# One half of a score tile in every fourth block goes from ScalarE's exponential to GpSimd's power

## The chip, the cores and the metric

The kernel runs on one core of one Trainium2 chip. A core has five engines that each work through their own queue in order: TensorE (PE in the profile, with PEld for its weight loads), VectorE (DVE), ScalarE (ACT), GpSimd (POOL) and SyncE (SP), which here only issues DMAs. They wait for one another through semaphores. The metric is the device time of one execution in microseconds (us); lower is better.

## What is computed

Two branches read the same `x` (2048 rows of 512 numbers) and are mixed row by row with a sigmoid gate. Branch A is attention with 32 heads of width 16 that share one key and one value; branch B is a SwiGLU feed-forward layer of width 1792. All data are float32.

```
g = _sigmoid((x * gate_w).sum(-1, keepdims=True))
# A: attention
q = (x @ wq).reshape(B, S, 32, 16) ; k = x @ wk ; v = x @ wv
scores = einsum("bhqd,bkd->bhqk", q, k) * (Dh ** -0.5)
p = softmax(scores) ; a = einsum("bhqk,bkd->bhqd", p, v) @ wo
# B: feed-forward
b = (silu(x @ w_gate) * (x @ w_up)) @ w_down
return g * a + (1 - g) * b
```

Branch A needs one exponential for each of 32 x 2048 x 2048 scores. The kernel takes no maximum off the scores first; a bound on them is checked at the end, and a slower path that takes the maximum is entered only where the bound fails.

## The kernel before

**Stages.** A first stage (to about 50 us) transposes `x`, makes keys, values and the first queries. The main stage (to about 1260 us) runs attention and, interleaved with it on TensorE, the rest of the projections and the feed-forward. A last stage multiplies by `wo` and mixes the branches.

**Units and tiles of attention.** A unit `u` is one head and one piece of 128 keys (512 units, 16 to a head). Its scores against all 2048 queries are two score tiles, `j` = 0 and 1, of 128x1024 in PSUM (`pss`, two buffers, two banks each). Each becomes half of the unit's tile `pt` (128x2048, SBUF). `score` issues the two matmuls of a score tile (L660). `exps` exponentiates with ScalarE (L668, scale 0.25). `mix` multiplies a whole `pt` by the values and a column of ones and adds into `po` (L680); the ones give the softmax's denominator.

**Blocks.** From unit 32 on the work goes in blocks of four units (`block`, k = 8 to 127). In block k the score tiles of units 4k+2 to 4k+5 are made, numbered i = 0 to 7, and then units 4k to 4k+3 are mixed. So units 4k+4 and 4k+5, tiles 4 to 7, are mixed only at the end of the next block. The order of a block is written out by hand: `STEPS` says where a score tile (S) and where a step of the feed-forward (F) stands on TensorE; an F is a matmul on the lower 64 rows of the array beside one on the upper 64 rows.

**Staged halves.** `KINDS = "AHHAHAAA"` says how each of the eight tiles is exponentiated. An A tile goes from PSUM through ScalarE in one instruction of 128x1024. Of an H tile (i = 1, 2, 4) ScalarE takes the first 512 columns from PSUM ("d" in `EXPS`), while VectorE copies the other 512 raw scores from PSUM into `pt` (L664), so that PSUM comes free early; ScalarE later exponentiates that staged half in place, `pt<-pt` ("s" in `EXPS`). `EXPS = ("0d", "1d", "2d", "3d", "4d", "5d", "1s", "4s", "2s", "|", "6d", "7d")` is ScalarE's order; at "|" stand the tanh of the feed-forward, if one is due.

**The other engines.** VectorE also evacuates the feed-forward's results (`pf`), multiplies them together in SBUF (L284, L298), splits them into a rounded and a remainder part (`split`, L106 and L107), and after each head normalizes its output (L689 and L692). GpSimd does one thing in this stage: it splits every weight tile that a DMA has brought (`wraw`) into two parts, a cast (L106) and a subtraction (L107). It waits for the DMA and for the matmuls that still read the buffer. SyncE issues all DMAs in program order.

Of the kernel before, what the change touches and what calls it, by code (L numbers as in the profile page):

```python
# [1 line left out]

# [6 lines left out]
F32 = mybir.dt.float32  # L9
# [4 lines left out]
ALU = mybir.AluOpType  # L14
# [4 lines left out]
P = 128  # L19
# [7 lines left out]
CH = 512  # L27
# [7 lines left out]
SCALE = DH ** -0.5  # L35
# [13 lines left out]
BLOCK = 4  # L49
# [13 lines left out]
def tile_gated_mix(ctx, tc, x, wq, wk, wv, wo, w_gate, w_up, w_down, gate_w, out):  # L63
    nc = tc.nc
# [3 lines left out]
    cpool = ctx.enter_context(tc.tile_pool(name="cpool", bufs=1))  # L68
# [55 lines left out]
    def run(queue, n):  # L124
        for _ in range(min(n, len(queue))):
            queue.pop(0)()
# [506 lines left out]


    PO, LATER = [], []
    hp = tc.alloc_tile_pool(name="hp", bufs=2)
    with tc.tile_pool(name="bpool", bufs=2) as bp:
        PT = {}
# [14 lines left out]
        def score(u, j, half=False):  # L653
            h, kt = divmod(u, NT)
            if j == 0:
                new_pt(u)
            ps = ps_s.tile([P, 2 * CH], F32, name="pss")
            for b in range(2):
                rows = slice(b * RT, (b + 1) * RT)
                nc.tensor.matmul(ps[:, b * CH:(b + 1) * CH], ks[rows, kt * P:(kt + 1) * P], QS[h][rows, j, :],  # L660
                                 start=True, stop=True)
            halves.clock += 1
            pt = PT[u][:, j * 2 * CH:(j + 1) * 2 * CH]
            other = nc.vector.tensor_copy(pt[:, CH:], ps[:, CH:]) if half else None  # L664
            return pt, ps, other

        def exps(pt, ps, other=None, w=slice(None)):
            ins = nc.scalar.activation(pt[:, w], ps[:, w], AF.Exp, scale=SCALE)  # L668
            if other is not None:
                tc.declare_no_dep(getattr(ins, "ins", ins), getattr(other, "ins", other), reason="another bank")  # L670

        def mix(u):
            h, kt = divmod(u, NT)
            pt = PT.pop(u)
            if kt == 0:
                run(COPY, 1)
                PO[:] = [ps_o.tile([P, CH], F32, name="po")]
            po = PO[0]
            for c in range(NCH):
                nc.tensor.matmul(po[c * 2 * DH:(c + 1) * 2 * DH, :], vaug[:, kt, :], pt[:, c * CH:(c + 1) * CH],  # L680
                                 start=(kt == 0), stop=(kt == NT - 1))
            if kt == NT - 1:

                osb = hp.tile([P, CH], F32, name="osb")
                rsb = hp.tile([P, CH], F32, name="rsb", bufs=1)

                def invert(i):
                    w = slice(i * P, (i + 1) * P)
                    nc.vector.reciprocal(rsb[:, w], rsb[:, w])  # L689

                def store():
                    nc.vector.tensor_tensor(osb, osb, rsb, ALU.mult)  # L692
                    for c in range(NCH):
                        nc.sync.dma_start(o_d[h * DH:(h + 1) * DH, c * CH:(c + 1) * CH],
                                          osb[c * 2 * DH:c * 2 * DH + DH, :])

                assert not LATER
                COPY.append(lambda: nc.vector.tensor_copy(osb, po))
                LATER.extend([(0.8, lambda: nc.vector.stream_shuffle(rsb, osb, [DH] * 2 * DH))] +
                             [(1.0, lambda i=i: invert(i)) for i in range(TC)] + [(0.8, store)])  # L700
# [5 lines left out]
        def feed(k, more=True):  # L706
            for _ in range(k):
                if JOBS and more or halves.busy():
                    halves.step(more)

        def block(k, first, last, steps, kinds, order):
            more = k < NB - STOP
            tiles = [(u, j) for u in range(first, last) for j in range(2)]
            order = list(order)
            made = []

            def emit():
                while order and order[0] != "|" and int(order[0][0]) < len(made):
                    i, how = int(order[0][0]), order.pop(0)[1]
                    pt, ps, other = made[i]  # L720
                    if how == "s":
                        exps(pt, pt, w=slice(CH, None))
                    else:
                        exps(pt, ps, other, slice(0, CH) if kinds[i] == "H" else slice(None))

            for i, what in enumerate(steps):
                if what == "F":
                    if "S" in steps[i + 1:i + 3] and kinds[len(made):len(made) + 1] == "H":
                        HOLD.append(i)
                    feed(1, more)  # L730
                    HOLD.clear()
                elif len(made) < len(tiles):
                    made.append(score(*tiles[len(made)], kinds[len(made)] == "H"))
                    emit()
                    run(EVAC, len(EVAC))
                if len(made) > 4:
                    run(COPY, 1)
            if order:
                order.pop(0)
            run(ACTS, len(ACTS))  # L740
            emit()
            assert not order and len(made) == len(tiles)
            left = BUDGET
            rest = NT // BLOCK - k % (NT // BLOCK)
            for _ in range(-(-len(LATER) // rest) if DEFER else 2):
                if LATER:
                    cost, f = LATER.pop(0)
                    left -= cost
                    f()
            for last in (False, True):  # L750
                kept = set()
                for item in list(DEFER):
                    n, cost, f = item
                    if n in kept or (n in FRESH) != last or cost > left:
                        kept.add(n)
                    else:
                        DEFER.remove(item)
                        left -= cost
                        f()
            FRESH.clear()  # L760
            for u in range(BLOCK * k, BLOCK * (k + 1)):
                mix(u)
            halves.clock += 2 * LONG
# [92 lines left out]
    with tc.If(rv != 0):  # L856
        with tc.tile_pool(name="gpool", bufs=2) as gp:
            with tc.For_i(0, H, 1) as h:
# [3 lines left out]
                for qt in range(NT):  # L862
# [17 lines left out]
                    for b in range(NT // TC):  # L880
                        pt = ps_f.tile([P, CH], F32, name="pf")
# [48 lines left out]
```

## Time and profile before

| | |
|---|---|
| median of 2 runs (lowest to highest) | 1343.7 us (1343.49 to 1343.92) |
| the profiled execution, its own time | 1344.01 us |
| span of its instructions | 1341.9 us |
| VectorE, share of the span busy | 54% |
| ScalarE | 79% |
| GpSimd | 29% |
| GpSimd, instructions | 408 |

The profiled execution's own time is 2.1 us more than the span between its first and its last instruction. A row of a group gives the busy time of all its instructions, the mean of one in nanoseconds, then the time its engine sat idle before them and what ended it. A row of the timeline gives start, length, engine, line, operation, output and inputs, shape, the number of instructions merged, and in brackets the idle time before. Where one instruction's end overlaps the next one's start, the row shows both.

### The profile page before, as it was taken

What the parts mean: (1) busy time and instruction counts of PE and PEld (TensorE: products, weight loads), DVE (VectorE), ACT (ScalarE), POOL (GpSimd) and SP (SyncE); (2) the same over time, 40 slices, a digit from 0 to 9 for tenths busy, and PEclk for the clock granted to TensorE, in tenths of its full rate; (3) what the DMA queues carried; (4) which work ended last, traced back from release to release, by engine and by line L of the source; (5) the groups of instructions that cost most, each with busy time, mean ns of one, the idle gap of its engine ahead of it and who ended that gap; (6) DMA issues with size and microseconds to landing.
All of it is one profiled execution on the core that took longest, in us unless ns stands there. A gap on an engine that the chain in (4) does not pass through costs nothing. (4 is left out here: it accounts for less than half of the span.)

```text
span 1341.9 us, 26802 instructions
## 1 busy us (share of the span) xinstructions
PE 1328.0 (99%) x10743; PEld 770.4 (57%) x10743; DVE 722.4 (54%) x1221; ACT 1061.6 (79%) x1463; POOL 391.0 (29%) x408
## 2 busy tenths in 40 slices
PE   9999999999999999999999999999999999999997
PEld 7655555555555555555555555555555555555576
DVE  5554565555455555555464555455454565465432
ACT  4578888888888888888888888888888888888400
POOL 6140321152042151152131241142131241333343
PEclk9999999999999999999999999999999999999999
DMA  8455221131122221141131221231121221222154
GB/s 277 142 173 190 65 60 38 35 107 44 44 86 77 78 80 38 35 107 44 52 122 39 82 79 39 57 83 45 52 61 30 81 79 39 74 68 60 44 161 143
DMA packets 101489, 107.79 MB, mean 80 GB/s; under 512 B 9968, under 2 KB 69616, under 8 KB 99696
## 3 DMA queue, kind: packets, MB, share of 16 engines
q1 hardware_dynamic: 99632, 105.81, 27.5%
q8 instruction: 88, 1.44, 0.5%
q10 hardware_dynamic: 1728, 0.20, 0.1%
q14 instruction: 41, 0.34, 0.1%
HBM read 76.09 MB, written 29.36 MB: 79 GB/s over the span
## 5 line engine op out<-in xcount | busy, mean ns | idle before, releaser
L668 ACT ACTIVATE pt<-pss 128x1024 f32<-128x1024 f32 (+1 forms) x1024 | 842.0, 876 | 177.3 <-PE pss L660 146.3
L664 DVE COPY pt<-pss 128x512 f32<-128x512 f32 x354 | 244.8, 692 | 415.6 <-PE pss L660 380.6
L680 PE MATMUL po<-pt,vaug 128*32 128x512 f32 x4096 | 467.6, 595 | 0.0
L660 PE MATMUL pss<-qs,ks 64*128 64x512 f32 x2048 | 403.1, 417 | 1.1 <-ACT pt L668 1.1
L660 PEld LDWEIGHTS pss<-qs,ks 64*128 64x128 f32 x2048 | 193.7, 184 | 218.4 <-ACT pt L668 183.6
L680 PEld LDWEIGHTS po<-pt,vaug 128*32 128x32 f32 x4096 | 119.2, 109 | 260.2 <-issue 255.2
L668 ACT ACTIVATE pt<-pt 128x512 f32<-128x512 f32 x354 | 195.7, 620 | 0.0
L176 PE MATMUL pf<-xh,wgl 64*128 64x512 f32 (+1 forms) x440 | 162.0, 392 | 0.0
L176 PE MATMUL pf<-xh,wgh 64*128 64x512 f32 (+1 forms) x440 | 160.5, 391 | 0.5 <-DVE acc L331 0.2
L176 PE MATMUL pf<-xl,wgh 64*128 64x512 f32 (+1 forms) x440 | 160.2, 390 | 0.0
L176 PE MATMUL pf<-xh,wuh 64*128 64x512 f32 (+1 forms) x440 | 158.4, 391 | 0.7 <-DVE sign L403 0.3
L176 PE MATMUL pf<-xl,wuh 64*128 64x512 f32 (+1 forms) x440 | 158.2, 390 | 0.0
L176 PE MATMUL pf<-xh,wul 64*128 64x512 f32 (+1 forms) x440 | 157.3, 391 | 0.0
L106 POOL CAST wgh<-wraw 128x512 fp32r<-128x512 f32 x56 | 36.1, 644 | 402.6 <-PE pf L176 311.8
L176 PE MATMUL pf<-wdh,hh 64*128 64x512 f32 (+1 forms) x427 | 143.4, 391 | 1.7 <-DVE hh L106 1.7
L176 PE MATMUL pf<-wdh,hl 64*128 64x512 f32 (+1 forms) x427 | 144.1, 390 | 0.0
L176 PE MATMUL pf<-wdl,hh 64*128 64x512 f32 (+1 forms) x427 | 143.4, 390 | 0.0
L689 DVE RECIPROCAL rsb<-rsb 128x128 f32<-128x128 f32 x128 | 117.1, 935 | 10.1 <-issue 8.2
L106 POOL CAST wuh<-wraw 128x512 fp32r<-128x512 f32 x56 | 35.1, 626 | 298.2 <-PE pf L176 245.3
L176 PEld LDWEIGHTS pf<-xh,wgh 64*128 64x128 f32 (+1 forms) x440 | 78.5, 185 | 9.8 <-issue 2.5
L176 PEld LDWEIGHTS pf<-xh,wuh 64*128 64x128 f32 (+1 forms) x440 | 77.3, 185 | 9.3 <-issue 3.7
L176 PEld LDWEIGHTS pf<-xl,wgh 64*128 64x128 f32 (+1 forms) x440 | 78.5, 185 | 6.0
(157 smaller groups left out, 1547.6 us busy)
## 6 DMA issues: line engine op xcount, KB each, us to landing
wraw<-in_B_w_gate_dram SPq DMA_DIRECT2D x56, 256.0 KB
wraw<-in_B_w_up_dram SPq DMA_DIRECT2D x56, 256.0 KB
wraw<-in_B_w_down_dram SPq DMA_DIRECT2D x56, 256.0 KB
qs<-q_d SPq DMA_DIRECT2D x62, 192.0 KB
q_d<-hl SPq DMA_DIRECT2D x18, 256.0 KB
q_d<-hh SPq DMA_DIRECT2D x18, 256.0 KB
o_d<-osb SPq DMA_DIRECT2D x128, 32.0 KB
a_d<-acc SPq DMA_DIRECT2D x4, 1024.0 KB
```

The lines of the kernel that those rows point to most:

```text
L106: eng_hi.tensor_copy(hi, src)
L176: ins = nc.tensor.matmul(self.ps, a, b, start=(i == 0 and not half), stop=(last and half != 0))
L660: nc.tensor.matmul(ps[:, b * CH:(b + 1) * CH], ks[rows, kt * P:(kt + 1) * P], QS[h][rows, j, :], start=True, stop=True)
L664: other = nc.vector.tensor_copy(pt[:, CH:], ps[:, CH:]) if half else None
L668: ins = nc.scalar.activation(pt[:, w], ps[:, w], AF.Exp, scale=SCALE)
L680: nc.tensor.matmul(po[c * 2 * DH:(c + 1) * 2 * DH, :], vaug[:, kt, :], pt[:, c * CH:(c + 1) * CH], start=(kt == 0), stop=(kt == NT - 1))
L689: nc.vector.reciprocal(rsb[:, w], rsb[:, w])
```

## The change

A column `base` of 128 numbers, each e to the power SCALE (SCALE is 0.25), is made once. In blocks with k % 4 == 1 the staged half of tile 4 is no longer exponentiated by ScalarE; GpSimd raises `base`, read again for every column, to the power of the raw score: (e^0.25)^s = e^(0.25 s).

```diff
+import math
...
     PO, LATER = [], []
+    base = cpool.tile([P, 1], F32, name="base")
+    nc.vector.memset(base, math.exp(SCALE))
...
                     i, how = int(order[0][0]), order.pop(0)[1]
                     pt, ps, other = made[i]
-                    if how == "s":
+                    if how == "s" and i == 4 and k % BLOCK == 1:
+                        nc.gpsimd.tensor_tensor(pt[:, CH:], base.to_broadcast([P, CH]), pt[:, CH:], ALU.pow)
+                    elif how == "s":
                         exps(pt, pt, w=slice(CH, None))
```

This comes to 30 instructions (k = 9, 13, ... 125). The line numbers of the changed kernel are higher: by 1 up to the memset, by 3 in `score` and `mix`, and by more after that. On ScalarE 30 of the rows `ACTIVATE pt<-pt 128x512` are gone, always the middle one of three, and nothing else moves there. VectorE has one row more, the memset. SyncE's rows are the same.

GpSimd's queue around block k = 69, before the change (`wgh`, `wgl`, `wuh`, `wul` are the two parts of a gate and of an up weight tile, `wraw` what the DMA brought):

```order
L106 CAST wgh_8188<-wraw_8186 128x512 [waits DMAHW6_49,PE_49]
L107 TENSOR_TENSOR wgl_8189<-wraw_8186,wgh_8188 128x512 [waits PE_49,Pool_49]
L106 CAST wuh_8281<-wraw_8279 128x512 [waits DMAHW3_49,PE_49]
L107 TENSOR_TENSOR wul_8282<-wraw_8279,wuh_8281 128x512 [waits PE_49,Pool_49]
L106 CAST wgh_8372<-wraw_8370 128x512 [waits DMAHW4_49,PE_49]
L107 TENSOR_TENSOR wgl_8373<-wraw_8370,wgh_8372 128x512 [waits PE_49,Pool_49]
```

And the same place with the change:

```order
L107 CAST wgh_8190<-wraw_8188 128x512 [waits DMAHW6_49,PE_49]
L108 TENSOR_TENSOR wgl_8191<-wraw_8188,wgh_8190 128x512 [waits PE_49,Pool_49]
L107 CAST wuh_8283<-wraw_8281 128x512 [waits DMAHW3_49,PE_49]
L108 TENSOR_TENSOR wul_8284<-wraw_8281,wuh_8283 128x512 [waits PE_49,Pool_49]
L725 TENSOR_TENSOR pt_8297<-base_629,pt_8297 128x512 [waits DVE_49,Activation_49]
L107 CAST wgh_8374<-wraw_8372 128x512 [waits DMAHW4_49,PE_49]
L108 TENSOR_TENSOR wgl_8375<-wraw_8372,wgh_8374 128x512 [waits PE_49,Pool_49]
```

The power stands between the split of one weight tile and that of the next, and waits for VectorE's copy of the raw scores into `pt_8297`.

TensorE's queue where the same tile is mixed, one block later (k = 70), before the change; the rows on `pss` are the last scores of that block, those on `po` the mix:

```order
L660 MATMUL pss_8434<-qs_7781,ks_78 128x512 [waits Activation_49]
L660 MATMUL pss_8434<-qs_7781,ks_78 128x512
L680 MATMUL po_8225<-pt_8295,vaug_79 32x512 x4
L680 MATMUL po_8225<-pt_8324,vaug_79 32x512 x4
L680 MATMUL po_8225<-pt_8353,vaug_79 32x512 x3
```

And with the change:

```order
L663 MATMUL pss_8436<-qs_7783,ks_78 128x512 [waits Activation_49]
L663 MATMUL pss_8436<-qs_7783,ks_78 128x512
L683 MATMUL po_8227<-pt_8297,vaug_79 32x512
L683 MATMUL po_8227<-pt_8297,vaug_79 32x512 [waits Pool_49]
L683 MATMUL po_8227<-pt_8297,vaug_79 32x512 x2
L683 MATMUL po_8227<-pt_8326,vaug_79 32x512 x4
```

The second matmul of the mix now waits for GpSimd; the rows are otherwise the same. Two blocks later the first ScalarE and the first VectorE instruction that write into the same buffer of `pt` wait for GpSimd as well, behind this mix.

## The prediction

> **What bounds the kernel now.** I read the page first, then the waits, then two neighbouring blocks by stretch and in order of time. The page's busy times:
>
> ```profile
> PE 1328.0 (99%) x10743; PEld 770.4 (57%) x10743; DVE 722.4 (54%) x1221; ACT 1061.6 (79%) x1463; POOL 391.0 (29%) x408
> ```
>
> A busy TensorE is not yet a bound, so I look at who waits for whom where a block begins. The view of waits, and two blocks (k = 68 and 69) as stretches; the columns of the stretches are length, then busy time and instruction count of PE, PEld, DVE, ACT and POOL, then clock, DMA share and GB/s:
>
> ```profile
> PEld pss L660 <- ACT pt L668: 183.6, 537, 1.4
> ACT pt L668 <- PE pss L660: 146.3, 164, 3.3
> 704.04:713.40 9.36, 9.36 (x83) 5.09 (x81) 6.35 (x10) 8.45 (x14) 3.81 (x4) 1.00 0.29 68
> 713.40:722.83 9.43, 9.43 (x82) 5.33 (x80) 5.00 (x10) 7.96 (x13) 1.90 (x2) 1.00 0.01 2
> ```
>
> The same blocks in order of time, first ScalarE, then TensorE's scores and mixes:
>
> ```profile
> 708.15 4.75 ACT L668 ACTIVATE pt<-pss 128x1024 f32<-128x1024 f32 x6 [0.70 <-PE pss L660]
> 712.80 1.66 ACT L668 ACTIVATE pt<-pt 128x512 f32<-128x512 f32 x3
> 714.36 1.93 ACT L668 ACTIVATE pt<-pss 128x1024 f32<-128x1024 f32 x2
> 717.51 4.82 ACT L668 ACTIVATE pt<-pss 128x1024 f32<-128x1024 f32 x6 [1.23 <-PE pss L660]
> 713.40 3.64 PE L680 MATMUL po<-pt,vaug 128*32 128x512 f32 x32
> 716.97 0.73 PE L660 MATMUL pss<-qs,ks 64*128 64x512 f32 x4
> 719.17 0.41 PE L660 MATMUL pss<-qs,ks 64*128 64x512 f32 x2
> 722.83 1.07 PE L680 MATMUL po<-pt,vaug 128*32 128x512 f32 x8
> ```
>
> At the end of a block ScalarE is through with its last two tiles at 716.29 (714.36 + 1.93) while TensorE mixes until 717.04. ScalarE then stands idle until TensorE brings new scores, 1.23 us here, and 0.70 us one block earlier, which has one instruction more on ScalarE (14 against 13, a tanh). That block is no longer for it: 9.36 against 9.43 us. So TensorE's queue sets a block, and 183.6 us that weight loads spend behind ScalarE lie under matmuls still running: TensorE is busy for the whole of both stretches.
>
> **What leaves ScalarE.** Three staged halves take 1.66 us, so one takes about 0.52 us net of the overlap of ends and starts (1.93 for two A tiles shows the same overlap). 30 of them are 30 x 0.52 = 15.6 us of ScalarE. It stands directly in front of tiles 6 and 7, whose PSUM the next block's first scores need; these come 0.52 us sooner, and ScalarE's idle time of 0.70 to 1.23 us grows by as much. Gain: 0. If that idle time were not there, it would be 15.6 us, 1.2%.
>
> **What GpSimd gets.** No power is in the trace. The nearest rows of the same shape on GpSimd, and two of VectorE that differ only in how hard the arithmetic is:
>
> ```profile
> L107 POOL TENSOR_TENSOR wdl<-wraw,wdh 128x512 fp32r<-128x512 f32 x56 | 75.4, 1347 | 4.5
> L664 DVE COPY pt<-pss 128x512 f32<-128x512 f32 x354 | 244.8, 692 | 415.6 <-PE pss L660 380.6 <-ACT pt L668 30.6
> L689 DVE RECIPROCAL rsb<-rsb 128x128 f32<-128x128 f32 x128 | 117.1, 935 | 10.1 <-issue 8.2 <-DVE pt L664 0.2
> ```
>
> Lower end: a power as cheap as a subtraction, 1.3 us. A reciprocal takes 935/128 = 7.3 ns a column, a copy 692/512 = 1.35, a ratio of 5.4. One hard function on GpSimd would by that ratio be 5.4 x 1.3 = 7.0 us. A power of floats is a logarithm, a product and an exponential, so two hard functions: 14.0 us, the value I take. Upper end: some 23 multiply-adds (ten and eight for two series good to float32, five to split and join exponents), each as dear as that subtraction: 23 x 1.3 = 30 us.
>
> **Where it lies.** VectorE's and GpSimd's rows around block 69, with the next block's first copies:
>
> ```profile
> 711.20 0.69 DVE L664 COPY pt<-pss 128x512 f32<-128x512 f32 x1
> 712.98 0.89 DVE L689 RECIPROCAL rsb<-rsb 128x128 f32<-128x128 f32 x1
> 713.79 0.36 DVE L106 CAST hh<-ht 128x512 fp32r<-128x512 f32 x1
> 714.19 0.69 DVE L107 TENSOR_TENSOR hl<-ht,hh 128x512 fp32r<-128x512 f32 x1
> 717.77 0.69 DVE L664 COPY pt<-pss 128x512 f32<-128x512 f32 x1 [2.89 <-PE pss L660]
> 710.25 1.30 POOL L107 TENSOR_TENSOR wul<-wraw,wuh 128x512 fp32r<-128x512 f32 x1
> 718.01 0.61 POOL L106 CAST wgh<-wraw 128x512 fp32r<-128x512 f32 x1 [6.46 <-PE pf L176]
> ```
>
> Tile 4's raw half is there at 711.89 (711.20 + 0.69), GpSimd is free since 711.55, and ScalarE's own half of the tile ends at about the same time (five of six tiles from 708.15). The power begins at 711.9. Its reader is the mix at 722.83: a cover of 10.9 us. At 14.0 us that alone would be a stall of 3.1.
>
> But VectorE and GpSimd disturb each other already. A pair on each engine:
>
> ```profile
> 693.85 0.69 DVE L296 TENSOR_TENSOR ht<-hs,pf 128x512 f32<-128x512 f32 x1 [0.62 <-PE pf L176]
> 694.46 1.73 DVE L692 TENSOR_TENSOR osb<-osb,rsb 128x512 f32<-128x512 f32 x1
> 694.35 1.30 POOL L107 TENSOR_TENSOR wul<-wraw,wuh 128x512 fp32r<-128x512 f32 x1
> L692 DVE TENSOR_TENSOR osb<-osb,rsb x32: 683/691/1794, 114.9 to 1275.7; 128x512 f32<-128x512 f32 x32
> 542.18 1.45 DVE L106 CAST hh<-ht 128x512 fp32r<-128x512 f32 x1
> 542.05 1.30 POOL L107 TENSOR_TENSOR wul<-wraw,wuh 128x512 fp32r<-128x512 f32 x1
> ```
>
> L692 reads two tiles in SBUF and takes 0.69 us at its median; begun 0.11 us behind a GpSimd subtraction it takes 1.73 and ends at 696.19, 0.54 after GpSimd has ended (695.65). The cast from SBUF to SBUF (0.36 above) takes 1.45 beside one and ends 0.28 after it. L296, with one input in PSUM, runs its 0.69 undisturbed. So a VectorE operation of the first kinds does not share: it waits for GpSimd's instruction to end. All of VectorE queues behind it, the score copies included.
>
> The Trainium skill has a rule for this (SBUF — State Buffer, "Who interferes with whom"): the pair of ports shared by the two engines is an exclusive lock, and whoever starts first keeps it for the whole instruction, however long. The three late ends above agree, though none of those holders is longer than 1.3 us; the rule gives the sum below, its absence the first rival.
>
> With a power of T, the cast due at 713.79 ends at 711.9 + T + 0.3, the subtraction 0.7 later, and only then come the copies. The first is due at 717.77, so T up to 4.8 is free; TensorE misses that copy only at 719.17, when it wants the buffer back, and the copy would have ended at 718.46: some 0.6 more, 5.4. In the 30 blocks I find such an operation inside the cover 23 times. The first and the last place, and one in which the operation is L284:
>
> ```profile
> 148.44 0.69 DVE L284 SCALAR_TENSOR_TENSOR ht<-ht,hs 128x512 f32<-128x512 f32 x1 [1.04 <-ACT ht L276]
> 752.72 0.69 DVE L284 SCALAR_TENSOR_TENSOR ht<-ht,hs 128x512 f32<-128x512 f32 x1
> 755.48 0.69 DVE L664 COPY pt<-pss 128x512 f32<-128x512 f32 x1 [2.07 <-PE pss L660]
> 1205.51 0.36 DVE L106 CAST hh<-ht 128x512 fp32r<-128x512 f32 x1
> ```
>
> In about eight of the 30 blocks a split still runs on GpSimd when the raw half is there, by up to 2 us; averaged in, 5.0 us of T are free at these 23 places, and 10.9 at the other 7.
>
> **The sum.** Stall = 23 x (T - 5.0) + 7 x (T - 10.9). At 14.0 us: 23 x 9.0 = 207, and 7 x 3.1 = 22, together 229 us. At 7.0: 46 us. At 30: 575 + 134 = 709. The split behind the power, at 718.01, comes 7.9 us late at 14.0; its reader on TensorE is late by 9.0 already, so nothing is added. The memset is one row at the start. ScalarE's idle time covers a late VectorE no further, since scores are then missing. The profiled execution has 1341.9 us of span and 2.1 around it, 1344.0, against a median of 1343.7: 1344.0 + 229 = 1573.
>
> **The rivals.** *Ports are not held* through a long instruction, because GpSimd reads in pieces between which VectorE slips in. Then only the mix waits: 30 x 3.1 = 93, so 1437. Against it stands that none of the late ends above came before GpSimd's. 0.07.
>
> *The power is cheap*, the other side: under about 6 us it costs less than 27 us (23 x 1.2 = 27.6 at T = 6.2), and under 5.0 nothing: 1344. For it speaks that 29% busy leaves GpSimd the room, and that its engine may do several steps a column. The Trainium skill (GPSIMD Engine Reference, section 3.1) counts about three operations per cycle for bodies of three or more; 23 by that rule are eight cycles a column, an estimate of 3.3 us. Its section 7 speaks the other way, four cycles for each step of a dependent chain: 23 x 4 cycles x 512 columns, an estimate of 39 us. No row here shows either. 0.14.
>
> *The power is far dearer* than 30 us, its chain worked through with little overlap; at 39, 23 x 34 + 7 x 28.1 = 979, so 2323. 0.18.
>
> *ScalarE is the hidden pace* and its 15.6 us count in full: 1328. Against it stand the idle times of 0.70 and 1.23. 0.01.
>
> **How the numbers follow.** The forecast, a power between 6.2 and 30 us with the ports held, has the remaining 0.60: 1372 to 2053, likeliest 1573. The range takes in the cheap power and its scatter below (1339) and stops at 2053; left out are the far dearer power and the pace of ScalarE, 0.19. Two per cent, 27 us, is about what a measurement of this kernel can tell from no change. Slower by more: 0.60 + 0.07 + 0.18 = 0.85. Within: 0.14. Faster by more: 0.01, since even 15.6 us are not 27.
>
> **What would show it.** A group of 30 powers on GpSimd with a mean near 14.0 us; VectorE rows of casts, L285 and L108 with a longest value of about that; every fourth block longer by about 9; idle time of TensorE's scores put down to VectorE's copy, and only a little of the mix's to GpSimd; 324 rows `pt<-pt` on ScalarE with more idle time in front of the tiles. Wrong would be the cost if the mean is outside 6 to 30; wrong the lock if VectorE's two-input rows stay below 2 us beside a power that lasts longer.

## The result, and the profile after

| | before | after |
|---|---|---|
| median of 2 runs | 1343.7 us | 3557.68 us |
| lowest to highest | 1343.49 to 1343.92 | 3556.36 to 3558.99 |
| span of the profiled execution | 1341.9 us | 3554.2 us |
| mean granted TensorE clock | 0.999 | 0.702 |

The changed kernel takes 2.6444 times as long (95% interval 2.638 to 2.6508). The forecast said slower and gave 1573 us, at most 2053; the direction came true and the size did not.

The page of the changed kernel: busy times, then the granted clock in 40 equal slices (9 is full speed), then the groups of instructions that answer to those shown of before:

```profile
PE 1427.1 (40%) x10743; PEld 785.9 (22%) x10743; DVE 719.2 (20%) x1222; ACT 1045.8 (29%) x1433; POOL 2844.5 (80%) x438
...
PEclk9966677666776667765777657776577765777669
...
L725 POOL TENSOR_TENSOR pt<-base,pt 128x512 f32<-128x512 f32 x30 | 2457.6, 81920 | 81.1 <-DVE pt L667 67.6
...
L683 PE MATMUL po<-pt,vaug 128*32 128x512 f32 x4096 | 561.9, 664 | 2040.8 <-POOL pt L725 2040.8
...
L177 PE MATMUL pf<-xh,wuh 64*128 64x512 f32 (+1 forms) x440 | 159.8, 395 | 73.5 <-POOL wuh L107 72.9
L671 ACT ACTIVATE pt<-pt 128x512 f32<-128x512 f32 x324 | 180.0, 620 | 0.0
```

One power of 128x512 takes 81.92 us. The forecast's term was 14.0, with 30 as its upper end. TensorE now stands still for 2040.8 us in front of mixes (L683; L680 before), and 30 of ScalarE's `pt<-pt` are gone, as the change intends. The waits, as total, number of times, and longest:

```profile
DVE pt L667 <- PE pss L663: 2453.3, 249, 78.9
ACT pt L671 <- PE pss L663: 2223.2, 162, 76.1
...
PE po L683 <- POOL pt L725: 2040.8, 29, 72.1
```

VectorE and ScalarE wait for TensorE's scores, TensorE waits for GpSimd, and of the waits of its matmuls less than 4 us in all are put down to VectorE. That is not the picture the forecast drew, in which VectorE was to be the engine waited for. The first power (block k = 9) in order of time, GpSimd, VectorE, then TensorE's mixes:

```profile
145.85 81.95 POOL L725 TENSOR_TENSOR pt<-base,pt 128x512 f32<-128x512 f32 x1
...
147.69 0.69 DVE L285 SCALAR_TENSOR_TENSOR ht<-ht,hs 128x512 f32<-128x512 f32 x1 [0.51 <-ACT ht L277]
...
155.62 0.36 DVE L107 CAST hh<-ht 128x512 fp32r<-128x512 f32 x1
156.02 0.69 DVE L108 TENSOR_TENSOR hl<-ht,hh 128x512 fp32r<-128x512 f32 x1
...
156.05 1.04 PE L683 MATMUL po<-pt,vaug 128*32 128x512 f32 x2
227.85 6.05 PE L683 MATMUL po<-pt,vaug 128*32 128x512 f32 x30 [70.76 <-POOL pt L725]
```

L285, a cast and L108 run inside the power at their undisturbed 0.69, 0.36 and 0.69 us. TensorE issues the first two rows of the mix, waits 70.76 us, and then the other 30 rows take 6.05 us, where all 32 took 3.64 before. Why they are slow shows in stretches of the same trace, cut at the start of the work after the wait:

```profile
145.00:228.00 83.00, 12.24 (x102) 6.59 (x102) 6.97 (x13) 12.35 (x17) 83.00 (x3) 0.60 0.01 3
228.00:231.00 3.00, 3.00 (x16) 0.64 (x16) 0.00 (x0) 0.00 (x0) 2.19 (x3) 0.50 0.03 8
231.00:234.00 3.00, 3.00 (x20) 0.67 (x14) 0.00 (x0) 0.00 (x0) 0.00 (x0) 0.71 0.28 80
234.00:237.00 3.00, 3.00 (x26) 2.12 (x27) 1.98 (x3) 2.46 (x4) 1.29 (x1) 1.00 0.00 0
```

The columns are those of the stretches in the prediction; the clock granted to TensorE is the number behind GpSimd's busy time. It is 0.50 in the first 3 us of work after the wait, 0.71 in the next, 1.00 from the third on.

The 2212.3 us of added span are then nearly all in three places of TensorE's queue: 2040.8 in 29 waits for a power at the mix; 561.9 - 467.6 = 94.3 in mixes that take longer; and 72.9 in two waits of feed-forward matmuls for a weight tile `wuh`, 72.6 of them for the tile queued behind the one power that is left, the 21st of the 30. They add up to 2208.0. The 467.6 is the mix's row on the page before:

```profile
L680 PE MATMUL po<-pt,vaug 128*32 128x512 f32 x4096 | 467.6, 595 | 0.0
```

### The profile page after: what moved, and what is told of

It reads as the page before. It is cut to its first block, busy times and chain, and to the rows that moved or that the text cites. A ratio compares the mean times of both kernels' runs of the same rounds, so it can differ in the third digit from the quotient of the medians.

```text
span 3554.2 us, 26829 instructions
## 1 busy us (share of the span) xinstructions
PE 1427.1 (40%) x10743; PEld 785.9 (22%) x10743; DVE 719.2 (20%) x1222; ACT 1045.8 (29%) x1433; POOL 2844.5 (80%) x438
## 5 line engine op out<-in xcount | busy, mean ns | idle before, releaser
L725 POOL TENSOR_TENSOR pt<-base,pt 128x512 f32<-128x512 f32 x30 | 2457.6, 81920 | 81.1 <-DVE pt L667 67.6
L671 ACT ACTIVATE pt<-pss 128x1024 f32<-128x1024 f32 (+1 forms) x1024 | 841.7, 876 | 2405.1 <-PE pss L663 2223.2
L683 PE MATMUL po<-pt,vaug 128*32 128x512 f32 x4096 | 561.9, 664 | 2040.8 <-POOL pt L725 2040.8
L683 PEld LDWEIGHTS po<-pt,vaug 128*32 128x32 f32 x4096 | 132.7, 120 | 2380.7 <-POOL pt L725 2067.1
L177 PE MATMUL pf<-xh,wuh 64*128 64x512 f32 (+1 forms) x440 | 159.8, 395 | 73.5 <-POOL wuh L107 72.9
L671 ACT ACTIVATE pt<-pt 128x512 f32<-128x512 f32 x324 | 180.0, 620 | 0.0
L108 POOL TENSOR_TENSOR wgl<-wraw,wgh 128x512 fp32r<-128x512 f32 x56 | 73.3, 1309 | 21.7 <-PE pf L177 17.3
```

The costliest lines, as they stand in the source:

```text
L108: eng.tensor_tensor(lo, src, hi.bitcast(F32), ALU.subtract)
L177: ins = nc.tensor.matmul(self.ps, a, b, start=(i == 0 and not half), stop=(last and half != 0))
L725: nc.gpsimd.tensor_tensor(pt[:, CH:], base.to_broadcast([P, CH]), pt[:, CH:], ALU.pow)
```

## The experiments

All edits are against the changed kernel. Ratios are to the kernel before, run on the same chip; it took medians of 1345.4 to 1346.5 us there.

**Is ScalarE's relief worth anything by itself?** In `e1_relief` the 30 staged halves are exponentiated by nobody.

```diff
                     if how == "s" and i == 4 and k % BLOCK == 1:
-                        nc.gpsimd.tensor_tensor(pt[:, CH:], base.to_broadcast([P, CH]), pt[:, CH:], ALU.pow)
+                        pass
```

> Leaves out the exponential of 30 staged halves altogether: ScalarE loses 30 x 0.52 = 15.6 us, GpSimd gets nothing. If TensorE sets every block (ScalarE idle 0.70 to 1.23 us at each start): 1344, within 3 us of before, and ScalarE's idle time ahead of its tiles up by about 15. If ScalarE is the hidden pace: 1328.

It took 1345.95 us, ratio 1.0004 (0.9992 to 1.0016). ScalarE's wait for scores in this run:

```profile
ACT pt L671 <- PE pss L663: 162.4, 166, 3.3
```

Before, this wait was 146.3. It grew by 16.1 us, about the 15.6 that were taken off ScalarE, so all of the gain turned into waiting. In `relief_all` tile 4's staged half is left out in every block of the main stage, 118 in place of 30:

```diff
-                    if how == "s" and i == 4 and k % BLOCK == 1:
-                        nc.gpsimd.tensor_tensor(pt[:, CH:], base.to_broadcast([P, CH]), pt[:, CH:], ALU.pow)
+                    if how == "s" and i == 4:
+                        pass
```

> Leaves out the exponential of tile 4's staged half in every block, 118 or 119 of them: ScalarE loses some 62 us and GpSimd gets nothing. This is the most that moving this half off ScalarE could bring with any helper that costs nothing. If TensorE sets every block: no change, within 4 us of before. If ScalarE sets the pace of part of the blocks: up to 62 us less, 1284.

It took 1346.43 us, ratio 1.0008 (0.9997 to 1.0019).

```profile
PE 1330.6 (99%) x10743; PEld 774.3 (58%) x10743; DVE 721.2 (54%) x1222; ACT 1000.0 (74%) x1345; POOL 391.2 (29%) x408
...
ACT pt L671 <- PE pss L663: 207.8, 165, 3.3
```

207.8 - 146.3 = 61.5 us of new waiting for 118 x 0.52 = 61.4 us taken off. Nearly four times the relief is worth as little: TensorE stays 99% busy.

**Is it the arithmetic, or the form and place of the instruction?** `e2_mult` keeps engine, operands, place and waits, and multiplies. The result no longer stands for the exponential.

```diff
-                        nc.gpsimd.tensor_tensor(pt[:, CH:], base.to_broadcast([P, CH]), pt[:, CH:], ALU.pow)
+                        nc.gpsimd.tensor_tensor(pt[:, CH:], base.to_broadcast([P, CH]), pt[:, CH:], ALU.mult)
```

> GpSimd multiplies the 30 halves by the same column, read again for every column, instead of raising it to a power; the exponentials are left out. If the power itself is what costs: the 30 rows at about 1.3 us, as the subtractions, and 1344. If the operand read again, the place in the queue or the new waits cost: the rows far above 1.3 us, or TensorE idle in front of the mix, and a time above 1371.

It took 1347.1 us, ratio 1.0002 (0.9992 to 1.0011).

```profile
L725 POOL TENSOR_TENSOR pt<-base,pt 128x512 f32<-128x512 f32 x30 | 31.3, 1042 | 79.4 <-DVE pt L667 66.3 <-DVE sign L404 13.0
```

A product with the broadcast operand takes 1.04 us. The new waits, the place in the queue and the operand form cost nothing measurable; the arithmetic is the cost.

**What does the power's time go by?** `cols64` and `cols128` give GpSimd 64 or 128 of the 512 columns and ScalarE the others; `rows64` gives it 64 of the 128 rows.

```diff
-                        nc.gpsimd.tensor_tensor(pt[:, CH:], base.to_broadcast([P, CH]), pt[:, CH:], ALU.pow)
+                        nc.gpsimd.tensor_tensor(pt[:, CH:CH + 64], base.to_broadcast([P, 64]), pt[:, CH:CH + 64], ALU.pow)
+                        exps(pt, pt, w=slice(CH + 64, None))
```

> GpSimd's power takes 64 of the 512 columns, ScalarE the other 448. At 81.9/512 = 0.160 us a column it lasts 10.2 us. If only the mix waits for it (cover 10.9, less at the eight places where a split still runs): about 6 us in sum, 1350. If VectorE is held for the whole power (5.0 free at 23 places): 23 x 5.2 = 120, 1464. If a power has a large fixed part, it lasts far over 10.2 and the time is above 1500.

The profiled run took 1359.53 us, two others 1358.15 and 1360.11, ratio 1.009 (1.0062 to 1.0117). A fourth took 3363.5; it has no trace, and the ratio leaves it out. Its mean granted clock was 1.000, where the runs with long waits of TensorE have 0.70 to 0.72, so it does not look like such waits; what happened in it stays open.

```profile
L725 POOL TENSOR_TENSOR pt<-base,pt 128x64 f32<-128x64 f32 x30 | 315.8, 10527 | 79.5 <-DVE pt L667 66.4 <-DVE sign L404 13.0
```

At 10.5 us the power fits under the cover of 10.9 us up to the mix, and the stall is nearly gone: TensorE waits for it in 3 of the 30 blocks, 1.5 us together. What is left is a loss of 13 us where about 6 was expected. The mixes account for 5.1 of it (472.7 us against 467.6), those waits for 1.5, and two waits for a weight tile split behind a power for 3.5; some 3 us stay open.

> GpSimd's power takes 128 columns, 20.5 us. If only the mix waits (mean cover 10.5): 30 x 10.0 = 300, 1644; with TensorE slower for a while after each wait, up to 3.3 us each, at most 1743. VectorE's operations with two inputs in SBUF keep to 1.8 us at most. If VectorE is held: 23 x 15.5 + 7 x 9.6 = 424, 1768, and such rows of over 10 us.

It took 1719.02 us, ratio 1.2761 (1.2728 to 1.2795).

```profile
L725 POOL TENSOR_TENSOR pt<-base,pt 128x128 f32<-128x128 f32 x30 | 621.6, 20720 | 81.1 <-DVE pt L667 67.5 <-DVE sign L404 13.5
L683 PE MATMUL po<-pt,vaug 128*32 128x512 f32 x4096 | 560.1, 662 | 265.4 <-POOL pt L725 265.4
...
860.12 1.04 PE L683 MATMUL po<-pt,vaug 128*32 128x512 f32 x2
869.75 6.05 PE L683 MATMUL po<-pt,vaug 128*32 128x512 f32 x30 [8.59 <-POOL pt L725]
881.69 3.64 PE L683 MATMUL po<-pt,vaug 128*32 128x512 f32 x32
```

The power's times of 10.53, 20.72 and 81.92 us for 64, 128 and 512 columns lie on a line of 0.33 us plus 0.159 a column. The mix is as slow after a wait of 8.59 us as after one of 70.76, and the next block's mix is back at 3.64: the slow rows come with each wait, not with its length. Of the 374.8 us by which the span grew (1716.7 against 1341.9), 265.4 are waits for the power, 92.5 longer mixes (560.1 - 467.6) and 11.9 waits for weight tiles. VectorE is not held: of its casts, L108, L285 and L695 that begin beside a power, at least 3 us before its end, none takes more than 0.70 us.

```diff
-                        nc.gpsimd.tensor_tensor(pt[:, CH:], base.to_broadcast([P, CH]), pt[:, CH:], ALU.pow)
+                        nc.gpsimd.tensor_tensor(pt[:RT, CH:], base[:RT].to_broadcast([RT, CH]), pt[:RT, CH:], ALU.pow)
+                        nc.scalar.activation(pt[RT:, CH:], pt[RT:, CH:], AF.Exp, scale=SCALE)
```

> The power takes all 512 columns of 64 of the 128 rows; ScalarE exponentiates the other 64 rows. If the time goes by columns, whatever the number of rows: 81.9 us an instruction and 3555, as with the change. If it goes by elements: 41 us, and about 1344 + 30 x (41 - 10.5) + 99 = 2358.

One run, 3555.45 us, next to the 3557.68 of the change:

```profile
L725 POOL TENSOR_TENSOR pt<-base,pt 64x512 f32<-64x512 f32 x30 | 2457.4, 81913 | 81.4 <-DVE pt L667 67.6 <-DVE sign L404 13.7
```

Half the rows take the same time. For these two numbers of rows the power goes by columns, not by elements.

**Is the mix's wait all that is lost?** In `scratch` ScalarE does all its exponentials, and GpSimd raises keys into a tile that nobody reads, so no mix waits for it.

```diff
+    spare = hp.tile([P, CH], F32, name="spare", bufs=1)
...
-                        nc.gpsimd.tensor_tensor(pt[:, CH:], base.to_broadcast([P, CH]), pt[:, CH:], ALU.pow)
+                        nc.gpsimd.tensor_tensor(spare, base.to_broadcast([P, CH]), ks[:, :CH].bitcast(F32), ALU.pow)
+                        exps(pt, pt, w=slice(CH, None))
```

> GpSimd raises the column to the power of 512 columns of ks into a spare tile that nobody reads, at the same places in its queue; ScalarE exponentiates all staged halves as before. So the mix has nothing to wait for, and only what else the queue carries counts. If GpSimd's queue is the next bound: about 30 x (81.9 + 9.5 of splits) = 2740 plus 145 ahead and 100 behind, 2990, with TensorE waiting for weight tiles. If only the mix's wait was the price: 1344.

It took 3183.45 us, ratio 2.365 (2.3581 to 2.3719).

```profile
PE 1410.9 (44%) x10743; PEld 806.6 (25%) x10743; DVE 714.6 (22%) x1222; ACT 1064.8 (33%) x1463; POOL 2839.2 (89%) x438
...
PE pf L177 <- POOL wuh L107: 1124.4, 19, 114.6
...
PE pf L177 <- POOL wgh L107: 540.0, 12, 73.4
```

With the mix freed, TensorE waits for weight tiles that GpSimd splits behind a power; GpSimd is busy for 89% of the span. Its 30 powers take 2458 us whatever reads them, so with the splits queued behind the powers as here, a later reader of the tile would win back about a tenth of the time at most. The run is some 190 us above the 2990 expected, which stays open. The power took as long on these other data (81933 ns in its group), so no dependence on the values shows.

**Does a long GpSimd instruction hold VectorE?** `longsub` gives GpSimd, at the power's place, a subtraction long enough to be told from those of before.

```diff
+    spare = hp.tile([P, 1408], BF16, name="spare", bufs=1)
...
-                        nc.gpsimd.tensor_tensor(pt[:, CH:], base.to_broadcast([P, CH]), pt[:, CH:], ALU.pow)
+                        nc.gpsimd.tensor_tensor(spare, ks[:, :1408].bitcast(F32), ks[:, :1408].bitcast(F32), ALU.subtract)
+                        exps(pt, pt, w=slice(CH, None))
```

> In place of the power GpSimd subtracts 1408 columns of ks from themselves into a spare tile (bf16), about 3.5 us; ScalarE does all exponentials. If a GpSimd instruction that streams its operands holds VectorE's two-input operations to its end: rows of VectorE beside it of up to about 4.0 us, ending 0.3 to 0.6 after GpSimd, and still 1344 to 1350 (5.0 us are free). If VectorE slips in between pieces: no row above 1.8.

It took 1348.11 us, ratio 1.0019 (1.0008 to 1.0031). Two places in order of time:

```profile
366.75 2.54 POOL L726 TENSOR_TENSOR spare<-ks 128x1408 bf16<-128x1408 f32 x1
...
367.29 2.55 DVE L285 SCALAR_TENSOR_TENSOR ht<-ht,hs 128x512 f32<-128x512 f32 x1
...
413.53 2.55 POOL L726 TENSOR_TENSOR spare<-ks 128x1408 bf16<-128x1408 f32 x1
...
413.71 2.64 DVE L107 CAST hh<-ht 128x512 fp32r<-128x512 f32 x1
```

The subtraction took 2.5 us, not the 3.5 I had expected, and did hold VectorE to its end: L285 ends at 369.84, 0.55 after GpSimd (369.29), and the cast at 416.35, 0.27 after it (416.08). All 16 operations that it caught show one of these two numbers within 0.02. The power is different. Over its 30 places in the changed kernel, 23 casts, 23 L108, 22 L285 and 12 L695 begin at least 3 us before its end, and the longest of any kind is 0.77 us. Three of them are lengthened: one cast by 0.06, 13 us into a power (in `cols128` it is as long), and two that begin right behind a power's start:

```profile
593.19 81.92 POOL L725 TENSOR_TENSOR pt<-base,pt 128x512 f32<-128x512 f32 x1
...
594.01 0.77 DVE L285 SCALAR_TENSOR_TENSOR ht<-ht,hs 128x512 f32<-128x512 f32 x1 [0.16 <-ACT ht L277]
...
928.07 81.92 POOL L725 TENSOR_TENSOR pt<-base,pt 128x512 f32<-128x512 f32 x1
...
928.74 0.66 DVE L107 CAST hh<-ht 128x512 fp32r<-128x512 f32 x1
```

They end at 594.78 and 929.40. Taking off the same 0.55 and 0.28, VectorE was released 1.04 and 1.05 us after the power's start, which is as long as the multiply of that form took in full. The traces of `scratch` (five operations) and `rows64` (one) have more of this kind, all released between 1.03 and 1.05 us. A cast of `scratch`:

```profile
1138.83 81.92 POOL L726 TENSOR_TENSOR spare<-base,ks 128x512 f32<-128x512 f32 x1
...
1139.38 0.78 DVE L107 CAST hh<-ht 128x512 fp32r<-128x512 f32 x1
```

It ends at 1140.16, 1.33 behind the power's start, and less 0.28 that is 1.05. With 128 columns the one cast that was caught (in `mixlast128`) was released after 0.40 us. So a power of 512 columns holds VectorE for its first 1.04 us or so and leaves it alone for the other 80.9. What it does with the ports in that time, no run shows.

**Is it the wait that makes the mix slow?** `busy128` is `cols128` with 40 matmuls that add zero, 8.8 us of work, put in front of each mix that waits.

```diff
+    zero = hp.tile([P, 2 * DH], F32, name="zero", bufs=1)
+    nc.vector.memset(zero, 0.0)
...
             for u in range(BLOCK * k, BLOCK * (k + 1)):
+                if k % BLOCK == 2 and u == BLOCK * k and k > 9:
+                    for _ in range(10):
+                        for c in range(NCH):
+                            nc.tensor.matmul(PO[0][c * 2 * DH:(c + 1) * 2 * DH, :], zero, PT[u + 1][:, c * CH:(c + 1) * CH],
+                                             start=False, stop=False)
                 mix(u)
```

> The version with 128 columns (20.7 us, 1719), and in front of each mix that waits for the power 40 more matmuls that add zeros into po, about 9.1 us, which is what TensorE waits there (265.4/29 = 9.2). If the 97 us that TensorE's busy time grew come from a clock that falls while it waits: the granted clock stays above 0.98 and the time falls to 1344 + 265 + 29 x 0.5 = about 1625, with more work done. If the clock has nothing to do with waiting: 1719 or more.

It took 1672.33 us, ratio 1.2424 (1.2388 to 1.246): 47 us less than `cols128`, with 264.8 us more work on TensorE.

```profile
L685 PE MATMUL po<-pt,vaug 128*32 128x512 f32 x4096 | 498.5, 597 | 18.4 <-POOL pt L727 18.4
L773 PE MATMUL po<-pt,zero 128*32 128x512 f32 x2400 | 264.8, 595 | 0.0
...
841.76 1.02 PE L685 MATMUL po<-pt,vaug 128*32 128x512 f32 x2
843.13 3.63 PE L685 MATMUL po<-pt,vaug 128*32 128x512 f32 x30 [0.35 <-POOL pt L727]
```

TensorE's idle time is filled and its mean clock is 0.993, against 0.915 in `cols128`; the 30 rows take 3.63 us in place of 6.05. So the slow mixes come from standing idle. Filling the wait does not bring its 8.8 us back, since the power ends when it ends; it takes away the slow restart behind it. What the clock does not explain is the cut: 1.02 + 3.63 us for a mix in two pieces, against 3.64 in one, about 1.0 us at each place. In an uncut mix the rows of a unit's four matmuls begin within 0.02 us of one another and run side by side, each row some 0.6 us long; the wait stands behind the first matmul, whose two rows then run alone. The span grew by 328.4 us (1670.3 against 1341.9): 264.8 of added work, 30.9 of longer mixes (498.5 - 467.6), nearly all from this cut, 18.4 of waits for the power that remain, and 14.3 of waits for weight tiles. The 1625 expected had 29 x 0.5 = 14.5 us beside the added work, where the last three come to 63.6.

**Does a later mix buy cover?** `mixlast128` is `cols128` with the waiting unit mixed last of its block's four.

```diff
-            for u in range(BLOCK * k, BLOCK * (k + 1)):
-                mix(u)
+            for n in range(BLOCK):
+                mix(BLOCK * k + (n + (k % BLOCK == 2)) % BLOCK)
```

> The version with 128 columns (20.7 us, 1719), and in the blocks behind a power the mix takes the unit with the power last instead of first, 2.7 us later (3 of 4 units of a mix of 3.64). If the wait of the mix is the price: TensorE's idle time in front of it falls from 265 to about 186 and the time to 1640. If the weight tiles queued behind the power set the pace, or VectorE: no change, 1719.

It took 1652.56 us, ratio 1.2284 (1.2259 to 1.2308).

```profile
PE po L683 <- POOL pt L725: 191.4, 29, 8.9
```

The wait fell from 265.4 to 191.4 us, by 74.0 / 29 = 2.55 us a place, about the three mixes (3.64 x 3/4 = 2.73) that now run first. The cover is what decides the stall. Within a block it can be lengthened by these 2.7 us, where the power of 81.9 us would need some 70.

## Why the prediction was right in direction and wrong in size

**The term that failed** is "What GpSimd gets": T = 14.0 us, from a ratio of 5.4 between a reciprocal and a copy on VectorE, taken twice. The power measured 81.92, 5.9 times the term and 2.7 times its upper end, which assumed 23 multiply-adds at 1.3 us each. The rows it was worked out from were rows of another engine, and of a subtraction on GpSimd; `e2_mult` shows that a multiply of the power's own form says as little, with 1.04 us. What in the power takes 0.16 us a column, no run shows. Of the rivals, *the power is far dearer* held on the size of T, though its price of 39 us was half of what came. The Trainium skill (GPSIMD Engine Reference, section 3.1) counts about three operations per cycle for bodies of three or more, an estimate of 3.3 us here; the trace has 25 times as much. Its section 7, an estimate of 39 us, is nearer and still less than half.

**The second step that failed** is "Where it lies": VectorE held for the whole power at 23 places. The late ends that I read it from were real (the lines show two of the three that the text counts), and `longsub` shows the same up to 2.5 us. They hold for a subtraction, and I carried them to an instruction that holds VectorE for its first 1.04 us only. The rival *ports are not held* was right for the power in what it makes of the time, and got 0.07; its reason, that VectorE slips in between pieces, no run shows. What the Trainium skill says (SBUF — State Buffer, "Who interferes with whom"), that the shared pair is kept for the whole instruction, agrees with `longsub` and not with the power of 81.9 us.

**What held.** With T = 81.9, and without the lock, the prediction's own terms give 30 x (81.9 - 10.9) = 2130 us. The cover of 10.9, read from one block, gives a wait of 71.0 a place; 2040.8 / 29 = 70.4 was measured at the 29 places where the mix waits, and 72.6 at the other, where the weight tile was waited for. With the lock the same formula would be 23 x 76.9 + 7 x 71.0 = 2266. With the 94 us of slower mixes, which the sum lacked, the version without the lock comes to 1344 + 2130 + 94 = 3568, 0.3% above the 3557.68 measured. So it was the size of one term that moved the total; the wrong lock would have moved it 136 us.

**ScalarE's relief** was forecast at 0, and `e1_relief` and `relief_all` bear it out, the second with 61 us taken off. **The split behind the power** was to add nothing. In the changed kernel that is so: at 29 places the mix waits and the split is behind in the same shadow, and at the other, the 21st in order, the split is what TensorE meets first, in place of the mix. At 81.9 us this has become true by luck of order only, since `scratch` shows that the split alone would hold the kernel at 3183 us.

**Of the signs named in advance,** the 324 rows on ScalarE and its longer waits came true, though in the changed kernel those waits (2223.2 us) are TensorE's stall, and only `e1_relief` and `relief_all` show the relief by itself. That TensorE's scores would wait for VectorE's copy, and the mix only a little for GpSimd, came out the other way round. The power's mean lies outside 6 to 30 us, which was to refute the cost, and VectorE's two-input rows stayed below 2 us beside a longer power, which was to refute the lock.

## What to carry to other kernels

Before moving work from one engine to another, ask whether the engine relieved waits for the bound: if its idle time grows by all that is taken off, as in `relief_all`, no price of the new place can pay. An operation that no trace shows is priced by a small dose of it first, since 64 columns under an 11 us cover would have told the price of 0.16 us a column for about 1% of the time, and neither another engine's ratio nor a count of steps came near. Interference read from one kind of instruction holds for that kind; see how long the new kind holds its neighbour before the interference is multiplied by its length.

## What the runs showed of the hardware that I had not expected

**A wait on TensorE costs more than its length.** After each wait for a power in the changed kernel the granted clock was 0.50 for some 3 us of work or more and back at 1.00 within about 6. In `busy128`, mixes after a remaining wait of 1.8 us or less took 3.63 us, and one after 3.31 us took 5.33; in `cols128` they took 4.9 to 6.6 after waits of 8.4 and more (the 30 rows behind the wait, in each case). In the changed kernel this is 94.3 us less the some 31 for the cut in two, an estimate of 63 us. The length of a short wait does not decide by itself whether the clock falls. In `cols64` it was 0.50 behind a wait of 2.23 us, and in `mixlast128` it stayed at 1.00 behind one of 2.74; each row is followed by a stretch behind it:

```profile
1197.03 0.79 PE L177 MATMUL pf<-xh,wuh 64*128 64x512 f32 x1 [2.23 <-POOL wuh L107]
1197.00:1200.00 3.00, 2.97 (x14) 2.16 (x16) 0.00 (x0) 1.71 (x3) 2.82 (x3) 0.50 0.31 99
...
1469.55 0.49 PE L177 MATMUL pf<-xh,wuh 64*128 64x512 f32 x1 [2.74 <-POOL wuh L107]
1470.00:1473.00 3.00, 2.61 (x26) 1.32 (x26) 0.00 (x0) 2.67 (x5) 2.70 (x3) 1.00 0.26 78
```

What else decides it, no run here tells. The Trainium skill (TensorE: Matmul & The Clock Gate, Part 1: The HAM clock gate) has about 3.4 us of idleness bring the clock to half, and about 3.4 us of work bring it back; the return within about 6 us is up to nearly twice the second figure, and the wait of 2.23 us is shorter than the first.

**A mix cut by a wait behind the first of its four side-by-side matmuls loses about 1 us** at full clock (1.02 + 3.63 against 3.64), even where the wait itself is 0.35.

**GpSimd's power takes 0.16 us for every column** of 64 or of 128 rows, and the same on scores as on keys, while a multiply of the same form takes 2.0 ns a column (1042 / 512): a factor of 79.
